# Held-back weight sums and the last turnings in the second product of a fused attention and feed-forward kernel

## Chip, core and metric

The kernel runs on one core of one Trainium2 chip. Its engines are TensorE (PE in the profile; PEld is its weight load), VectorE (DVE), ScalarE (ACT), GpSimd (POOL, "Pool" in the text) and SyncE (SP), which issues most DMAs. The metric is the device time of one execution in microseconds (us); the median over several executions is given. "Span" is the time that the profiler's record of one execution covers.

## What is computed

Hashed attention over 4 batches and 8 heads (768 positions, 64 numbers each), and then a feed-forward block on the 3072 rows of 512 numbers that come out. Only the second product of the feed-forward block bears on the change:

```python
def _moe_ref(x, w_in, w_out):            # x: 3072 x 512, from the attention
    h = x @ w_in                         # w_in: 512 x 2048
    g = h * (1.0 / (1.0 + np.exp(-1.702 * h)))
    return (g @ w_out).astype(np.float32)   # w_out: 2048 x 512
```

All inputs to these products are float32 (the weights come as float64 and are converted on the chip).

## The kernel before

**Stages.** Attention takes the first third of the span. Then `feed_forward` computes `x @ w_in` with the gelu (`hidden`, to about 614 us) and keeps the results in DRAM (`g_dram`), and then `g @ w_out`, from about 614 us to the end. The whole change lies in this last stage.

**Fewer multiplications.** Both products go by Strassen's scheme in Winograd's form, twice nested: a product of two 2 x 2 block matrices takes seven block products instead of eight, at the price of sums of blocks before and after. The outer scheme cuts `g @ w_out` into seven outer products, named by their number o in the order `OUTER = (1, 2, 6, 7, 5, 3, 4)`. The rows of x are taken in three super blocks of 1024 (`sb`), so the stage is a list `steps_out` of 21 products, counted n = 0 to 20 below. Each is again a product of two block matrices: seven inner products, each a group that shows as eight matmuls (128 x 256) in the trace and goes into one bank of PSUM, in the order 1, 2, 3, 6, 7, 5, 4 (in the last product 1, 3, 6, 7, 5, 2, 4). These groups are "L820" in the trace.

**Sums ahead of a product.** The scheme needs three sums and one overwritten block of each factor:

- of W_out: `inner_sums(at)` for the outer product OUTER[at], four sums (L211 to L214) of 128 x 512 on Pool. They are needed once, before product n = at; the products of the later super blocks use them again. The fourth result (L214) is the weight of inner product 3, the third group of its product. Those for at = 0 to 3 are made while `hidden` still runs; those for at = 4 to 6 during this stage.
- of g: `g_sums(n)`, four sums (L219 to L222) of 128 x 1024 on DVE, made during product n - 1 for product n: t1, then the block overwritten in place (raw_g or s_in), then t2, then t4. t2 is the moving factor of inner product 6, the fourth group (t2a for even n, t2b for odd n); t4 that of the last group.

**Sums behind a product.** `product_of_halves` (L809 to L853) emits the seven groups and takes their results out of PSUM: ScalarE copies groups 1 (`u`, L833) and 3 (L836), DVE adds the others (all adds are L824), and adds an earlier outer product's result where there is one (`acc`). Between them it calls `after(0)` to `after(3)` (`after(4)` in the last product alone), where the loop puts other work of DVE: pending additions and turnings, then the g sums of the next product: the first at 1, the second at 2, the last two at 3. For o = 3 an addition of two whole results (L957) comes ahead of the product, and another (L958) at `after(0)`.

**Turning and writing.** A finished result is turned in 32 x 32 blocks by DVE (`turned`, L800, one instruction for each of four quarters) into `y`, and `written` (L807) issues four DMAs from `y` to the output. In the last super block SP and ScalarE share these issues.

**Order.** The instructions of TensorE, DVE, ScalarE and Pool run in the order in which the code emits them; SP's order is set by a scheduler. The g blocks come by `fetch(n + 1)` (two DMAs of 1 MB on SP's queue, L775), issued during product n into the one of two buffers that product n - 1 has left.

**The marks.** Four times a copy of one element on Pool (L924) reads the result of the product before. It has no use for its value: Pool's queue waits there until that product's first DVE add is done, and so the sums behind it begin then:

```python
if 2 <= n <= 5:
    nc.gpsimd.tensor_copy(mark, ms[OUTER[n - 1]][0:1, 0, 0:1])
i = n % 2 * 2
for f in inner_sums(4) if n == 0 else inner_sums(4 + n // 2)[i : i + 2] if 2 <= n <= 5 else []:
    f()
```

So a mark emitted at n runs during product n - 1, and in the trace the marks of n = 2, 3, 4, 5 are at 637.46, 647.26, 658.06 and 669.18.

Of the kernel before, what the change touches and what calls it, by code (L numbers as in the profile page):

```python
# [38 lines left out]
def kernel(  # L39
# [113 lines left out]
    for x in (0x3FFFFFFF, 0xFF800000):  # L153
        m = const.tile([P, 1], U32, name=f"mask_{x:x}")
# [53 lines left out]
    def sums_a(eng, a11, a12, s3, a22, s1, s2, s4, a21=None):  # L208

        a21 = s3 if a21 is None else a21  # L210
        return [lambda: eng.tensor_tensor(s1, a21, a22, op=Alu.add),  # L211
                lambda: eng.tensor_tensor(s3, a11, a21, op=Alu.subtract),
                lambda: eng.tensor_tensor(s2, s1, a11, op=Alu.subtract),
                lambda: eng.tensor_tensor(s4, a12, s2, op=Alu.subtract)]  # L214
# [464 lines left out]
    def feed_forward(tag, late=()):  # L679
# [9 lines left out]
        with ExitStack() as fctx:  # L689
# [62 lines left out]
            def w_quarters(o):  # L752

                w = wqs[LEFT[o]]
                x = [w[:, i, F4 * j : F4 * (j + 1), :] for i in range(2) for j in range(2)]
                at = OUTER.index(o)
                if at == 0:
                    return x[0:2] + rooms[3:4] + x[3:] + rooms[0:3]
                return x + rooms[3 * at + 1 : 3 * at + 4]

            def inner_sums(at):

                if at == 0:
                    w = w_quarters(OUTER[0])
                    return sums_a(nc.gpsimd, *w, wqs[LEFT[OUTER[0]]][:, 1, 0:F4, :])
                return sums_a(nc.gpsimd, *w_quarters(OUTER[at])) if at < len(OUTER) else []
# [4 lines left out]
            def fetch(n):  # L771
                sb, o = steps_out[n]
                for h in range(2):
                    cs = slice(h * F4, (h + 1) * F4)
                    loader[0].dma_start(out=raw_g[n % 2][:, cs], in_=g_dram[len(LEFT) * sb + RIGHT[o], :, cs, :])  # L775
# [14 lines left out]
            def g_sums(n):  # L790
                return sums_b(nc.vector, *g_quarters(n)) if n < len(steps_out) else [lambda: None] * 4
# [3 lines left out]
            def turned(c, i, j, q0, q1):  # L795

                for q in range(q0, q1):
                    h, k = divmod(q, 2)
                    y = ys[j].rearrange("p b (d r) -> p r b d", r=4)[:, 2 * i + h, k * (TH // 32) : (k + 1) * (TH // 32), :]
                    nc.vector.transpose(y, c[:, q].rearrange("p (b t) -> p b t", t=32))  # L800

            def written(sb, j, halves, queues):
                first, last = halves[0] * TH, (halves[-1] + 1) * TH
                for a in range(4):
                    t0 = (2 * sb + j) * XT
                    dst = out[t0 + first : t0 + last, a * P : (a + 1) * P].rearrange("(b t) d -> t b d", t=32)
                    queues[a % len(queues)].dma_start(out=dst, in_=ys[j][32 * a : 32 * (a + 1), first // 32 : last // 32, :])  # L807

            def product_of_halves(n, acc, after):  # L809

                sb, o = steps_out[n]
                wq, gq = w_quarters(o), g_quarters(n)
                m = wholes[n % len(wholes)]
                u, v = (gp.tile([P, TH], F32, tag=x, name=x, bufs=2) for x in ("u", "v"))
                c11, c12, c21, c22 = (m[:, i] for i in range(4))

                def product(i):
                    ps = bank()[:, 0:TH]
                    for c in range(F4):
                        nc.tensor.matmul(ps, wq[LEFT[i]][:, c, :], gq[RIGHT[i]][:, c, :], start=(c == 0), stop=(c == F4 - 1))  # L820
                    return ps

                def add(dst, x, y):
                    nc.vector.tensor_tensor(dst, x, y, op=Alu.add)  # L824

                def corner():
                    add(c11, product(2), u)
                    if acc is not None:
                        add(c11, c11, acc[:, 0])


                final = n + 1 == len(steps_out)
                nc.scalar.copy(u, product(1))  # L833
                if not final:
                    corner()
                nc.scalar.copy(c12, product(3))  # L836
                after(0)
                add(v, product(6), u)
                add(c21, product(7), v)
                if acc is not None:  # L840
                    add(v, v, acc[:, 1])
                    add(c22, c21, acc[:, 3])
                    add(c21, c21, acc[:, 2])
                add(c12, c12, v)
                after(1)
                p = product(5)
                add(c22, p, c21 if acc is None else c22)
                add(c12, p, c12)
                after(2)
                if final:  # L850
                    corner()
                    after(4)
                add(c21, product(4), c21)  # L853
                after(3)
                return m

            def conversions(cv, psum, chunks):

                gens = [convert(cv, *x, psum=psum) for x in chunks]
                next(gens[0])  # L860
                for i, x in enumerate(gens):
                    for y in gens[i + 1 : i + 2]:
                        next(y)
                    for at, _ in enumerate(x):
                        if at == 2:
                            yield
                    yield

            MT = FC // 2
            for sb in range(n1):  # L870
                for mt in range(MT):
                    n = sb * MT + mt
                    if n == 1:
# [12 lines left out]
                        steps = conversions(cv, cps, late + chunks)  # L886
# [31 lines left out]
            for n, (sb, o) in enumerate(steps_out):  # L918
                final = n + 1 == len(steps_out)
                if 0 < n and n + 1 < len(steps_out):  # L920
                    fetch(n + 1)

                if 2 <= n <= 5:
                    nc.gpsimd.tensor_copy(mark, ms[OUTER[n - 1]][0:1, 0, 0:1])  # L924
                i = n % 2 * 2
                for f in inner_sums(4) if n == 0 else inner_sums(4 + n // 2)[i : i + 2] if 2 <= n <= 5 else []:
                    f()
                later_sums = g_sums(n + 1)
                m = wholes[n % len(wholes)]

                def after(at):
                    if at == 0:
                        while pending:
                            pending.pop(0)()

                    for f in later_sums[at : at + 1] if n == 0 else ([], later_sums[0:1], later_sums[1:2], later_sums[2:], [])[at]:
                        f()

                    if n + 2 >= len(steps_out):
                        for q in ((0,) * (not final), (), (1, 3), (2,), (0,))[at]:  # L940
                            turned(m, int(final), int(not final), q, q + 1)
                    if final and at in (2, 3):
                        written(sb, 0, (3 - at,), loader + [nc.scalar])
                    if n + 2 == len(steps_out) and at == 3:
                        written(sb, 1, (0, 1), loader + [nc.scalar])

                acc = {6: 1, 7: 6, 2: 1, 3: 6, 4: 7}.get(o)
                if o == 3:
                    pending.pop(0)()
                ms[o] = product_of_halves(n, None if acc is None else ms[acc], after)  # L950

                def flat(x):
                    return x.rearrange("p q t -> p (q t)")

                if o == 5:
                    m5, m6, m7 = (ms[i] for i in (5, 6, 7))
                    pending += [lambda a=m6, b=m5: nc.vector.tensor_tensor(flat(a), flat(a), flat(b), op=Alu.add),  # L957
                                lambda a=m5, b=m7: nc.vector.tensor_tensor(flat(a), flat(a), flat(b), op=Alu.add),  # L958
                                lambda a=m5: turned(a, 1, 1, 0, 4)]
                elif o in (2, 3) and n + 2 < len(steps_out):  # L960
                    pending.append(lambda a=ms[o], j=int(o == 3): turned(a, 0, j, 0, 4))
                    if o == 3:
                        pending.append(lambda sb=sb: written(sb, 1, (0, 1), loader))
                elif o == 4 and not final:
                    pending.append(lambda a=ms[4]: turned(a, 1, 0, 0, 4))
                    pending.append(lambda sb=sb: written(sb, 0, (0, 1), loader))
                yield
# [50 lines left out]
```

## Time and profile before

| what | value |
|---|---|
| median of 9 runs | 880.59 us (880.21 to 882.77) |
| profiled execution | 880.64 us, its span 878.8 us, granted TensorE clock 0.997 |
| busy over the span | PE 99%, DVE 82%, Pool 37%, ACT 36% |
| busy in 640 to 680 us | PE 38.05 of 40, DVE 33.22, Pool 8.46 |
| busy in 680 to 840 us | PE 160.00 of 160, DVE 128.85, Pool 0 |
| busy in 840 to 860 us | PE 20.00 of 20, DVE 17.74 |
| granted clock from 614 to 872 us | 1.00 |

A timeline line reads: start, duration, engine, line of the code, operation, output<-inputs, partitions x elements of output and input, how many such instructions in a row, and in brackets how long the engine had been idle before it and what ended that. Where a line merges several instructions ("x2"), the duration is from the first one's start to the last one's end. An instruction's record begins when its engine takes it up, so a duration can hold time in which it stands still. DMA issues are written with a q behind the engine (SPq, ACTq).

From 614 us TensorE's matmuls follow one another with two gaps, of 1.95 us and 0.82 us. A product of seven groups takes 12.09 us without a gap, a group 1.73 us. DVE's free durations in this stage are 1.22 us for a sum of 128 x 1024, 0.42 us for an add of 128 x 256, and 2.04 us for four transposes in a row; Pool's is 1.26 us for a sum of 128 x 512.

### The profile page before, as it was taken

The page shows a single profiled execution, that of the slowest core. Times are in us where ns is not written, and L with a number is a line of the kernel's source. Part 1 is how long each engine was busy: PE and PEld are TensorE (multiplying, and loading weights), DVE is VectorE, ACT ScalarE, POOL GpSimd, SP SyncE. Part 2 cuts the span into 40 slices and gives each one's busy share as a digit, 9 for nine tenths or more (in the row PEclk, how much of TensorE's full clock was granted, in tenths as well). Part 3 has the DMA queues.
Part 4 walks back from the last instruction along what each step waited for, and adds up shares of the span by engine and source line. Part 5 has one row for each costly group of instructions (what it writes and reads, how often), then busy time and mean ns, then how long its engine had stood idle before and what let it go on. Part 6 is the DMA issues. An engine that isn't in the chain of part 4 may idle for free.

```text
span 878.8 us, 11897 instructions
## 1 busy us (share of the span) xinstructions
PE 866.8 (99%) x4077; PEld 498.0 (57%) x4077; DVE 723.4 (82%) x1020; ACT 314.5 (36%) x519; POOL 322.1 (37%) x277
## 2 busy tenths in 40 slices
PE   9999999999999999999999999999999999999996
PEld 4444444444444444444444444444878888888885
DVE  4689989999999986787777787888897977897786
ACT  5767776776676642222232222332000000000000
POOL 4343343334433364675443344659931000000000
PEclk9999999999999999999999999999999999999998
DMA  6544545664444103555455645575835675467524
GB/s 132 95 62 85 104 82 99 100 102 84 83 82 97 56 0 133 214 195 203 165 186 197 215 163 196 199 246 178 303 133 187 200 219 209 157 221 239 192 96 100
DMA packets 169157, 132.01 MB, mean 150 GB/s; under 512 B 123616, under 2 KB 138112, under 8 KB 163712
## 3 DMA queue, kind: packets, MB, share of 16 engines
q1 hardware_dynamic: 166528, 129.70, 51.6%
q10 hardware_dynamic: 2560, 1.46, 0.8%
q8 instruction: 34, 0.56, 0.3%
q14 instruction: 35, 0.29, 0.1%
HBM read 79.69 MB, written 50.33 MB: 148 GB/s over the span
## 4 chain that ended last, share of the span: by engine, by line
PE 95%; DVE 4%; issue 0%; DVEq 0%
PE product L708 33%; PE product L820 25%; PE ps L432 18%; PE av L458 15%; PE dn L479 2%; DVE xT L824 2%; PE hash L408 1%; DVE y L800 1%; PE tp L366 1%; PE warm L359 0%; PE hash L373 0%; DVE v L824 0%; DVE t2a L221 0%; DVE raw_g L220 0%; DVE t4g L222 0%
## 5 line engine op out<-in xcount | busy, mean ns | idle before, releaser
L433 ACT ACTIVATE e<-ps 128x768 f32<-128x768 f32 x192 | 151.1, 812 | 15.0 <-PE ps L432 12.7
L432 PE MATMUL ps<-qT,kT 64*128 64x384 f32 x768 | 155.1, 482 | 0.0
L708 PE MATMUL product<-xT,w_in_sb 128*128 128x512 f32 x288 | 135.5, 593 | 0.0
L458 PE MATMUL av<-e,v 128*64 128x385 f32 x768 | 131.5, 490 | 0.0
L440 POOL TENSOR_TENSOR acc<-e 128x768 f32<-128x768 f32 x32 | 58.7, 1833 | 192.1 <-DVE acc L448 128.0
L716 ACT ACTIVATE c<-c 128x512 f32<-128x512 f32 x72 | 45.4, 630 | 186.9 <-issue 78.9
L458 PEld LDWEIGHTS av<-e,v 128*64 128x64 f32 x768 | 52.2, 136 | 76.4 <-issue 75.9
L708 PEld LDWEIGHTS product<-xT,w_in_sb 128*128 128x128 f32 x288 | 54.6, 190 | 69.1 <-issue 64.1
L708 PE MATMUL product<-t_x,s_in 128*128 128x512 f32 x192 | 90.2, 592 | 0.0
L432 PEld LDWEIGHTS ps<-qT,kT 64*128 64x128 f32 x768 | 68.1, 188 | 35.3 <-issue 35.3
L219 POOL TENSOR_TENSOR v<-c,u 128x512 f32<-128x512 f32 x24 | 34.2, 1424 | 123.2 <-ACT c L716 123.2
L833 ACT COPY u<-product 128x256 f32<-128x256 f32 x21 | 7.8, 372 | 173.9 <-PE product L820 132.3
L432 PE MATMUL ps<-qf,kf 64*128 64x384 bf16 x384 | 62.9, 324 | 0.1
L708 PEld LDWEIGHTS product<-t_x,s_in 128*128 128x128 f32 x192 | 36.5, 190 | 45.9 <-issue 43.8
L441 POOL TENSOR_TENSOR acc<-acc,e 128x768 f32<-128x768 f32 x32 | 59.1, 1847 | 2.5
L708 PE MATMUL product<-t_x,w_in_sb 128*128 128x512 f32 x96 | 45.1, 592 | 0.0
L708 PE MATMUL product<-xT,s_in 128*128 128x512 f32 x96 | 45.1, 592 | 0.0
L432 PEld LDWEIGHTS <-kf 64*128 64x128 bf16 x384 | 18.8, 94 | 41.3 <-issue 19.5
L446 DVE SCALAR_TENSOR_TENSOR acc<-e 128x768 f32<-128x768 f32 x32 | 32.2, 1007 | 5.1 <-ACT e L433 5.1
L469 ACT COPY vs<-av 128x1 f32<-128x1 f32 x32 | 5.1, 159 | 86.1 <-PE av L458 86.1
L820 PE MATMUL product<-raw_g,xT 128*128 128x256 f32 x152 | 35.1, 379 | 0.0
L448 DVE TENSOR_TENSOR acc<-acc,e 128x768 f32<-128x768 f32 x32 | 32.3, 1010 | 3.3
(208 smaller groups left out, 1543.6 us busy)
## 6 DMA issues: line engine op xcount, KB each, us to landing
raw_g<-g_dram SPq DMA_DIRECT2D x22, 1024.0 KB
s_in<-g_dram SPq DMA_DIRECT2D x20, 1024.0 KB
g_dram<-c SPq DMA_DIRECT2D x72, 256.0 KB
g_dram<-t SPq DMA_DIRECT2D x48, 256.0 KB
raw<-in_moe_w_in_dram SPq DMA_DIRECT2D x16, 512.0 KB
raw<-in_moe_w_out_dram SPq DMA_DIRECT2D x16, 512.0 KB
v<-in_v_dram SPq DMA_DIRECT2D x32, 192.0 KB
g_dram<-u SPq DMA_DIRECT2D x24, 256.0 KB
```

The costliest lines, as they stand in the source:

```text
L219: return [lambda: eng.tensor_tensor(t1, b12, b11, op=Alu.subtract), lambda: eng.tensor_tensor(b12, b22, b12, op=Alu.subtract), lambda: eng ...
L432: nc.tensor.matmul(ps[:, j, 0:HS], a[hs, keys], m[hs, cols], start=not last, stop=last)
L433: nc.scalar.activation(es[c][:, kt, :, 0:HS], ps[:, :, 0:HS], Act.Exp, scale=1.0 / D**0.5)
L440: nc.gpsimd.tensor_tensor(acc, es[c][:, 0, :, 0:HS], es[c][:, 1, :, 0:HS], op=Alu.add)
L441: nc.gpsimd.tensor_tensor(acc, acc, es[c][:, 2, :, 0:HS], op=Alu.add)
L446: nc.vector.scalar_tensor_tensor(acc, e[0], T * TINY, e[1], op0=Alu.add, op1=Alu.add)
L448: nc.vector.tensor_tensor(acc, acc, x, op=Alu.add)
L458: nc.tensor.matmul(av[D * j : D * (j + 1), :], vt[:, t, j, :], es[c][:, t, j, :], start=(t == 0), stop=(t == T - 1))
L479: nc.tensor.matmul(dn[r0 : r0 + 32, :], ones[:, 0:32], acc[:, j, :], start=True, stop=True)
L708: nc.tensor.matmul(ps, wq[LEFT[i]][:, kc, :], xq[RIGHT[i]][:, kc, :], start=(kc == 0), stop=(kc == K2 - 1))
L716: nc.scalar.activation(c, c, Act.Gelu_apprx_sigmoid)
L820: nc.tensor.matmul(ps, wq[LEFT[i]][:, c, :], gq[RIGHT[i]][:, c, :], start=(c == 0), stop=(c == F4 - 1))
```

## The change

```diff
-                if 2 <= n <= 5:
+                if n in (5, 6):
                     nc.gpsimd.tensor_copy(mark, ms[OUTER[n - 1]][0:1, 0, 0:1])
-                i = n % 2 * 2
-                for f in inner_sums(4) if n == 0 else inner_sums(4 + n // 2)[i : i + 2] if 2 <= n <= 5 else []:
+                for f in {0: inner_sums(4), 5: inner_sums(5) + inner_sums(6)[:2], 6: inner_sums(6)[2:]}.get(n, []):
                     f()
...
-                    for f in later_sums[at : at + 1] if n == 0 else ([], later_sums[0:1], later_sums[1:2], later_sums[2:], [])[at]:
-                        f()
+                    steps = [later_sums[at : at + 1]] if n == 0 else [[], later_sums[0:1], later_sums[1:2], later_sums[2:], []][at : at + 1]
+
+                    if n + 2 >= len(steps_out):
+                        turns = [lambda q=q: turned(m, int(final), int(not final), q, q + 1) for q in range(4)]
+                        if final:
+                            steps = [[[], [], [turns[1], turns[3]], [turns[2]], [turns[0]]][at]]
+                        elif at == 3:
+                            steps = [later_sums[2:3], turns[0:2], turns[3:4], later_sums[3:], turns[2:3]]
+                    for f in sum(steps, []):
+                        f()
 
-                    if n + 2 >= len(steps_out):
-                        for q in ((0,) * (not final), (), (1, 3), (2,), (0,))[at]:
-                            turned(m, int(final), int(not final), q, q + 1)
```

Two parts:

1. On Pool. The sums for OUTER[5] and OUTER[6] were made in pairs behind the marks of n = 2, 3, 4, 5. Now six of the eight stand behind the mark of n = 5 and the last two behind a mark of n = 6. The marks of n = 2, 3 and 4 are gone. The sums themselves are the same.
2. On DVE, in product 19 (the second but last). Its four turnings stood at `after(0)` (quarter 0), `after(2)` behind the second g sum (quarters 1 and 3), and `after(3)` behind the last g sum (quarter 2). Now all four are at `after(3)`: the third g sum (t2), quarters 0, 1 and 3, the fourth g sum (t4), quarter 2. The last product's turnings stay where they were.

The order of TensorE, ScalarE and SP is the same in both kernels.

## The prediction

> The products of the last stage are counted n = 0 to 20. Times with two decimals are microseconds from the start of the profiled span (878.8 us). Its execution took 880.64 us, so 1.8 us lie around the span; the median of the nine runs is 880.59, 0.05 lower.
>
> **What bounds the kernel now.** First the chain of waits, in order of time (start, us, engine):
>
> ```profile
> 613.99 20.73 PE product L820 x96
> ...
> 645.15 0.14 issue
> 645.29 197.09 PE product L820 x912
> ...
> 871.58 0.63 DVE y L800
> ```
>
> TensorE carries it, except from 634.7 to 645.3 and from 842.4 to the end, where it runs through DVE. TensorE's timeline prices both stretches:
>
> ```profile
> 645.29 1.97 PE L820 MATMUL product<-t2a,w_in_sb 128*128 128x256 f32 x8 [1.95 <-DVE t2a L221]
> ...
> 693.71 1.89 PE L820 MATMUL product<-t2a,s_in 128*128 128x256 f32 x8
> ...
> 862.19 1.99 PE L820 MATMUL product<-t2a,s_in 128*128 128x256 f32 x8 [0.82 <-DVE t2a L221]
> ```
>
> The first and third are TensorE's only waits in this stage. A product of seven groups takes 12.09 us (652.27 to 664.36); product 2 began at 638.00 and product 3 at 652.27, so the first wait costs 14.27 - 12.09 = 2.18. Around the other, groups begin at 859.47 and 864.02, 4.55 apart instead of 2 x 1.73: 1.09. Why t2a came late in product 2 is read from DVE's timeline and Pool's side by side:
>
> ```profile
> 636.31 3.02 DVE L824 TENSOR_TENSOR xT<-xT 128x256 f32<-128x256 f32 x2
> 639.26 1.49 DVE L824 TENSOR_TENSOR xT<-xT,v 128x256 f32<-128x256 f32 x1
> ...
> 643.94 1.21 DVE L221 TENSOR_TENSOR t2a<-raw_g,t1a 128x1024 f32<-128x1024 f32 x1
> ...
> 690.48 1.22 DVE L221 TENSOR_TENSOR t2a<-raw_g,t1a 128x1024 f32<-128x1024 f32 x1
> ```
>
> ```profile
> 636.18 1.33 POOL L214 TENSOR_TENSOR w_in_sb<-xT,w_in_sb 128x512 f32<-128x512 f32 x1
> 637.46 0.37 POOL L924 COPY mark<-xT 1x1 f32<-1x1 f32 x1
> 637.79 1.25 POOL L211 TENSOR_TENSOR w_in_sb<-xT 128x512 f32<-128x512 f32 x1
> 639.13 1.33 POOL L212 TENSOR_TENSOR xT<-xT 128x512 f32<-128x512 f32 x1
> ...
> 669.18 0.17 POOL L924 COPY mark<-t_x 1x1 f32<-1x1 f32 x1 [8.38 <-DVE t_x L824]
> ```
>
> The pair of adds at 636.31 took 3.02; the same pair at 650.33, with Pool idle, took 0.88. Each add ends about 0.3 after a Pool sum ends (637.51, 639.04, 640.46): a DVE sum of two SBUF tensors stands still while a Pool sum runs. It goes both ways: at 625.57 a Pool sum took 2.13 instead of 1.26, ending 1.27 after the DVE sum before it. They take turns, one whole instruction each. DVE adds that read a product from PSUM do not wait (the pair at 626.50: 0.74), nor do transposes (four at 647.12 beside two sums: 2.06; alone 2.04).
>
> **Part 1, the held-back sums.** Removed: two sums and a mark ahead of each of products 2, 3, 4, so with the added one four marks become two. The mark of product 5 stays and now leads six sums instead of two; a mark of product 6 with two sums is added. No DMA is issued more or less, and neither SP's nor ScalarE's order changes.
>
> Gain at product 2. L214 still ends at 637.51 and holds the first add; then Pool is empty. From the first add's end (637.85) the next ones go at their free pace: they start as if the pair had begun at 637.43, plus 0.79 (650.33 to 651.12), plus 0.34 (651.12 to 651.46), so t1a starts at 638.56 instead of 640.67, 2.11 earlier, and t2a ends at 645.15 - 2.11 = 643.04. TensorE wants it at 641.45 + 1.73 = 643.18 and takes it 0.06 to 0.14 after its end. The 2.18 go to 0, at most 0.1. From here all of TensorE is 2.18 earlier; DVE has waits for it of 1.38 and 1.30 in product 3, so it follows. The sums taken from 647.40 and 658.20 lay beside transposes and idle time, so taking them away is worth nothing.
>
> Cost at products 4 to 6. The mark now at 669.18 comes at 667.00. Six sums at a spacing of 1.30 start at 667.14, 668.47, 669.70, 671.04, 672.28, 673.62. DVE is idle or reading PSUM until 671.35, so three and a half sums are hidden by its waits of 2.35 and 1.30. Without that cover each costs up to 1.26. Then they take turns: the add c12 (673.53 before, now 671.35) waits for the fourth sum until 672.30; t1b waits for the fifth until 673.75 and ends 674.83; L220 waits for the sixth until 676.00 and ends 677.08, where it would have ended at 676.89 - 2.18 = 674.71. DVE is 2.37 late. The t2b wanted in product 5 at 681.62 - 2.18 = 679.44 ends at 678.35 - 2.18 + 2.37 = 678.54: in time. In product 5 the second mark waits for c11 (681.8); its two sums meet L958, which has already begun, and then transposes, so DVE loses nothing; they end by 685.4. DVE's only reserve there is its wait of 0.30 before 685.28. With it, DVE is back at the times it had before, and t2a of product 6 ends at 691.70 as now. But TensorE wants it at 693.71 - 2.18 = 691.53: a new wait of about 0.3, with the refill seen at 645.29 (1.97 instead of 1.89) 0.4. In product 7 DVE's idle 1.30 before 697.37 makes up the rest. Behind the marks only sums are queued, and TensorE waits for those: product 5 reads its fourth at 679.90 - 2.18 = 677.7 (done 672.3), product 6 its fourth at about 690 (done 685.4). One fetch is to be watched: the second half for product 8 stands in SP's queue behind four writes that wait for transposes, and these do not move; issued at 699.66, it is used at 710.13, then at 708.3; transfers run until about 706.3, so 2 us remain.
>
> Bounds of the new wait: nothing if Pool's sums start 0.4 earlier or DVE gains one turn; 1.8 if DVE loses the rest of all three sums, 3.8 in place of 2.37. I take 0.4, from the row-by-row turns.
>
> The Trainium skill speaks against bunching the sums: "SBUF — State Buffer", section "Who interferes with whom", has DVE instructions with two SBUF inputs contend with Pool's reads, whoever issues first holding the port for the whole instruction. The rows above agree on that lock, but show it changing hands after each instruction, which the page does not promise; if Pool kept it through its queue, the estimate would be 1.8 instead of 0.4.
>
> **Part 2, the turning of product 19.** Four transposes stay four. One of them leaves the batch of five at 851.92, two leave the place before t2a (859.66, 1.09 us); three come behind t2a. What DVE gains ahead of t2a: the batch of four frees v at 851.92 + 1.87 = 853.79 (1.87: 682.71 to 684.58) instead of 854.25, but the next add waits for its product until 854.50 (now 854.79), so 0.29; then 0.95 for the two (859.66 to 860.61): t2a ends near 860.92, before the 861.20 at which TensorE wants it. The 1.09 vanish from TensorE. But they do not reach the end, which ScalarE's timeline shows:
>
> ```profile
> 864.02 0.91 ACTq L807 DMA_DIRECT2D out_dram<-y  x2
> 865.03 0.37 ACT L833 COPY u<-product 128x256 f32<-128x256 f32 x1 [13.62 <-PE product L820]
> ```
>
> ScalarE copies u, the last product's first group, only after it has issued product 19's two writes, which wait for its last transpose; DVE's v at 865.43 waits for u. After that DVE runs to 872.21 with hardly a gap (0.1, for the group ending at 871.09). In the new order t2a at 859.70, three transposes at 0.47, t4 (1.14) and one transpose of 0.64 end at 864.14 instead of 863.95. So v comes at 865.62, and without the gap of 0.1 DVE ends at 872.3: +0.08. TensorE's 1.09 is hidden behind DVE. Bounds: -1.09 if the end followed TensorE; +0.4 if the writes, which keep the DMA engines at 0.9 and more from 865 to 875, pass their delay on twice. I take +0.1.
>
> **Sum.** 880.64 - 2.18 + 0.4 + 0.1 = 878.96; less 0.05 for the median: 878.9.
>
> **The rivals.**
> 1. No second wait: t2a of product 6 is in time. For it: 0.3 is small beside eight steps each known to 0.1. Against: DVE's chain from 671 to 691 has only 0.30 of idle. 880.6 - 2.18 + 0.1 = 878.5. Chance 0.15.
> 2. The end follows TensorE, u being out of the way: a further 1.09 + 0.1, so 877.7. Against: the order in ScalarE's queue is unchanged. 0.06.
> 3. Pool keeps the port: DVE 3.8 late, the new wait 1.8: 880.3, no change. For it: 3.02 at 636.31. Against: Pool's 2.13 at 625.57. 0.13.
> 4. Slower: the bunched sums hold DVE through products 4 to 6. If all eight block it in full, 8 x 1.26 = 10.1, less 0.30 of idle, it is 9.8 late; of this 1.87 is free at 691.70 (693.71 - 691.70 - 0.14), so the wait is 7.9: 880.6 - 2.2 + 7.9 + 0.1 = 886.4. It decides from the point where DVE is 5.8 late (1.87 + 2.18 + 1.76). For it: six sums in a row; against: half of them fall into idle time. 0.06.
>
> **How the numbers follow.** The forecast has 0.60; its own range, 878.3 to 879.6, comes from 0.1 to 0.9 for the new wait and 0 to 0.4 for the tail. A difference under 0.2% (1.76 us) is about what a measurement of this kernel can't tell from no change; the border is 878.83, and the forecast lies on it, so I split it in halves. Faster: 0.30 + 0.15 + 0.06 = 0.51. Within 0.2%: 0.30 + 0.13 = 0.43. Slower: 0.06. The range 878.0 to 880.3 leaves out most of rivals 2 and 4.
>
> **What would show it.** Right: no wait of TensorE near 643; the pair at 636.31 at about 1.9 us; six Pool sums from 667, the last three drawn out by DVE's; a short wait for t2a near 691.5; none near 861; DVE's v near the end still waiting for ScalarE's u. Wrong: a wait over 1 us between 675 and 705, or u copied before the writes are issued.

## The result, and the profile after

| | before | changed |
|---|---|---|
| median of the executions | 881.08 us (33 runs, 879.87 to 883.34) | 878.7 us (10 runs, 878.32 to 879.53) |
| ratio, 95% interval | | 0.997 (0.9962 to 0.9978) |
| profiled execution, span | 880.64 us, 878.8 us | 878.69 us, 876.9 us |
| first group of product 0 to u of product 19 | 233.81 us | 232.02 us |
| u of product 19 to the end of DVE's last instruction | 24.58 us | 24.48 us |
| from there to the end of the span | 6.59 us | 6.41 us |

The last three rows split the span behind the start of the stage into "stage", "tail" and "rest", which are used for all experiments below. In the changed kernel, profiled a second time, they are 232.03, 24.47 and 6.42. Between kernels that do not differ there, stage and tail repeat to 0.03 us; the rest repeats less well, it lies between 6.25 and 6.45 in eight profiles with the same order of turning and writing. Two executions far outside all others (1140.29 us of part 1 alone, at a granted clock of 0.753, and 3949.94 us of the kernel before) are left out everywhere. The stage is read from the start of the first L820 group to ScalarE's copy L833 in product 19, the tail from that copy to the end of the last L800. So the profile's 1.9 us are 1.79 of stage, 0.10 of tail and 0.18 of rest, less 0.17 by which this execution reached the stage later.

The chain of waits of the changed kernel, in order of time:

```profile
614.15 77.75 PE product L820 x360
691.90 0.12 issue
692.02 160.83 PE product L820 x744
...
862.43 0.37 ACTq L807
...
863.44 0.38 ACT u L833
...
869.86 0.63 DVE y L800
```

From 614 to 692 TensorE now carries it without DVE; what is left of a wait stands at 692. At the end ScalarE's DMA issues (ACTq) and its copy of u have come into the chain. TensorE's timeline at the three places where the prediction looked:

```profile
643.34 1.94 PE L820 MATMUL product<-t2a,w_in_sb 128*128 128x256 f32 x8
...
690.01 1.89 PE L820 MATMUL product<-raw_g,s_in 128*128 128x256 f32 x8
692.02 1.96 PE L820 MATMUL product<-t2a,s_in 128*128 128x256 f32 x8
...
859.58 1.89 PE L820 MATMUL product<-t2a,s_in 128*128 128x256 f32 x8
```

No bracket is left: the waits of 1.95 and 0.82 us are gone. A small one has come: after 690.01 the next group was due at 691.74 and starts at 692.02, and it takes 1.96 instead of 1.89. Product 2 now takes 650.29 - 638.16 = 12.13 us, product 6 takes 699.00 - 686.55 = 12.45, 0.36 over the free 12.09. DVE and Pool of the changed kernel, first where the wait was, then where the six sums meet DVE:

```profile
636.48 1.95 DVE L824 TENSOR_TENSOR xT<-xT 128x256 f32<-128x256 f32 x2
638.35 0.42 DVE L824 TENSOR_TENSOR xT<-xT,v 128x256 f32<-128x256 f32 x1
...
671.56 1.25 DVE L824 TENSOR_TENSOR t_x<-t_x,v 128x256 f32<-128x256 f32 x1
672.73 2.28 DVE L219 TENSOR_TENSOR t1b<-s_in 128x1024 f32<-128x1024 f32 x1
674.93 0.74 DVE L824 TENSOR_TENSOR t_x<-product,t_x 128x256 f32<-128x256 f32 x2
675.60 1.62 DVE L220 TENSOR_TENSOR s_in<-s_in 128x1024 f32<-128x1024 f32 x1
...
690.66 1.22 DVE L221 TENSOR_TENSOR t2a<-raw_g,t1a 128x1024 f32<-128x1024 f32 x1
```

```profile
667.21 0.17 POOL L924 COPY mark<-t_x 1x1 f32<-1x1 f32 x1 [29.51 <-DVE t_x L824]
...
671.26 1.26 POOL L214 TENSOR_TENSOR w_in_sb<-xT,w_in_sb 128x512 f32<-128x512 f32 x1
672.48 1.44 POOL L211 TENSOR_TENSOR w_in_sb<-w_out_sb 128x512 f32<-128x512 f32 x1
674.00 2.14 POOL L212 TENSOR_TENSOR w_out_sb<-w_out_sb 128x512 f32<-128x512 f32 x1
681.94 1.11 POOL L924 COPY mark<-t_x 1x1 f32<-1x1 f32 x1 [5.80 <-DVE t_x L824]
```

Read the ends: Pool's fourth sum ends at 672.52 and DVE's add at 672.81, Pool's fifth at 673.92 and t1b at 675.01, Pool's sixth at 676.14 and L220 at 677.22. The two engines take turns, one instruction each, while the adds at 674.93, which read PSUM, keep their 0.74.

The tail: first DVE's v in the kernel before, then DVE and ScalarE of the changed kernel:

```profile
865.43 0.42 DVE L824 TENSOR_TENSOR v<-product,u 128x256 f32<-128x256 f32 x1 [1.49 <-ACT u L833]
```

```profile
859.20 1.58 DVE L800 STREAM_TRANSPOSE y<-xT 128x256 f32<-128x256 f32 x3
...
863.85 0.43 DVE L824 TENSOR_TENSOR v<-product,u 128x256 f32<-128x256 f32 x1 [1.49 <-ACT u L833]
```

```profile
862.43 0.91 ACTq L807 DMA_DIRECT2D out_dram<-y  x2
863.44 0.37 ACT L833 COPY u<-product 128x256 f32<-128x256 f32 x1 [13.65 <-PE product L820]
```

The group that u is copied from has been ready since about 858, for 5 us. The copy waits behind two writes, these for the last turning (861.75 to 862.36), and DVE for the copy, for the same 1.49 us as before. TensorE's last group ends at 868.38, 2.1 us ahead of DVE (before: 1.1).

### The profile page after: what moved, and what is told of

Read it like the earlier page. It is cut to its first block, busy times and chain, and to the rows that moved or that the text cites. A ratio compares the mean times of both kernels' runs of the same rounds, so it can differ in the third digit from the quotient of the medians.

```text
span 876.9 us, 11895 instructions
## 1 busy us (share of the span) xinstructions
PE 866.4 (99%) x4077; PEld 497.8 (57%) x4077; DVE 723.1 (82%) x1020; ACT 314.8 (36%) x519; POOL 323.8 (37%) x275
## 4 chain that ended last, share of the span: by engine, by line
PE 96%; DVE 2%; DMA 1%; issue 0%; SPq 0%; ACTq 0%; ACT 0%; DVEq 0%
PE product L708 33%; PE product L820 27%; PE ps L432 18%; PE av L458 15%; PE dn L479 2%; PE hash L408 1%; DVE xT L824 1%; DMA q<-in_q_dram 1%; DVE y L800 1%; PE hash L373 0%; PE tp L366 0%; DVE v L824 0%; DVE t2a L221 0%; DVE raw_g L220 0%; ACTq L807 0%
## 5 line engine op out<-in xcount | busy, mean ns | idle before, releaser
L833 ACT COPY u<-product 128x256 f32<-128x256 f32 x21 | 7.8, 372 | 172.1 <-PE product L820 138.9
L820 PE MATMUL product<-raw_g,xT 128*128 128x256 f32 x152 | 35.1, 379 | 0.0
```

## The experiments

Every time in the lists "stage, tail, rest" is from one profile; before: 233.81, 24.58, 6.59, changed: 232.02, 24.48, 6.41.

**Each part alone.** The two parts of the diff do not touch each other's lines, so each was put into the kernel before by itself.

> The kernel before with the first part alone (Pool's sums in products 5 and 6; product 19 turned as before). Theory A (the whole gain is product 2's wait, less a new one in product 6): no wait of TensorE in product 2, about 0.3 us of wait ahead of inner product 6 of product 6, and the old wait of about 0.8 us in the last product; 1.7 to 1.9 us faster than before, so the same time as the changed kernel within 0.3 us. Theory B (part 2 carries a share of the gain): at least 0.5 us slower than the changed kernel.

> The kernel before with the second part alone (product 19 turned behind three of the last product's sums; Pool's sums as before). Theory A (ScalarE copies u only behind the two writes it issues, and these wait for the last turning): no wait of TensorE in the last product, but DVE's first add of inner product 6 there still waits for u and ends the chain; the span changes by less than 0.3 us. Theory B: TensorE's wait of 1.09 us reaches the end, 0.8 to 1.2 us faster than before.

Part 1 alone: 232.02, 24.57, 6.73; ratio to the kernel before 0.9971 (0.996 to 0.9983), that of the whole change within 0.0001. TensorE waits 0.81 us in the last product, as before, and 0.28 in product 6. Theory A holds.

Part 2 alone: 235.51, 24.48, 6.45; ratio 0.9999 (0.9987 to 1.0011). No wait of TensorE in the last product, and no gain of 0.8 us or more in the executions: theory B falls. The span of the profiled execution was to change by less than 0.3 us, but it is 2.0 us longer (880.8 against 878.8): it reached the stage 0.54 us later, and its stage, which part 2 does not touch, is 1.70 us longer. TensorE's timeline and the windows of one microsecond (the last three columns are granted clock, DMA share and GB/s) show why:

```profile
645.84 2.67 PE L820 MATMUL product<-t2a,w_in_sb 128*128 128x256 f32 x8 [1.96 <-DVE t2a L221]
648.30 2.92 PE L820 MATMUL product<-raw_g,xT 128*128 128x256 f32 x8
```

```profile
646.00:647.00 1.00, 1.00 (x5) 0.87 (x5) 1.00 (x2) 0.00 (x0) 0.00 (x0) 0.98 0.00 0
647.00:648.00 1.00, 1.00 (x4) 0.80 (x3) 0.97 (x3) 0.00 (x0) 0.19 (x2) 0.50 0.07 8
...
650.00:651.00 1.00, 1.00 (x5) 0.88 (x4) 0.00 (x0) 0.00 (x0) 0.57 (x1) 0.82 0.97 410
651.00:652.00 1.00, 1.00 (x7) 0.87 (x6) 0.71 (x2) 0.00 (x0) 0.00 (x0) 1.00 0.18 74
```

After the same wait of 1.96 us the granted clock falls to 0.50 from about 647.0 to 650.4. The clock lost in 646 to 651 is 0.02 + 3 x 0.50 + 0.18 = 1.70 us, the whole of the difference. In the kernel before's own profile it stays at 1.00 there. Six of part 2's twelve executions took over 881.9 us, against nine of the kernel before's 26 in the same rounds; the medians of those below are 880.03 and 880.36.

**Where the first pair stands.**

```diff
-                if n in (5, 6):
+                if n in (2, 5, 6):
...
-                for f in {0: inner_sums(4), 5: inner_sums(5) + inner_sums(6)[:2], 6: inner_sums(6)[2:]}.get(n, []):
+                for f in {0: inner_sums(4), 2: inner_sums(5)[:2], 5: inner_sums(5)[2:] + inner_sums(6)[:2], 6: inner_sums(6)[2:]}.get(n, []):
```

The other version has 4 in place of 2 in both lines.

> The changed kernel with the first two of the held-back sums back behind a mark of n = 2; the other six stay at n = 5 and 6. Theory A (these two sums alone hold DVE up in product 2): the wait of 1.9 us ahead of inner product 6 of product 2 is back, the wait in product 6 is gone since only four sums run from 669 on; 880.4 to 880.8 in one profile, as before the change. Rival (it is the marks, or the sums of n = 3 and 4, that cost): no wait in product 2, time as the changed kernel's.

> The changed kernel with the first two of the held-back sums behind a mark of n = 4, so that four instead of six stand behind that of n = 5. Theory A (DVE is late in product 6 because the last three of six bunched sums meet its own sums): DVE is about 0.9 instead of 2.0 us late after product 4's sums, no wait of TensorE in products 2 to 7, 0.3 to 0.4 us faster than the changed kernel. Rival (the wait in product 6 comes from the two sums behind the mark of n = 6, or from the late transposes): the wait of 0.3 us stays, and the time is the changed kernel's.

The pair at n = 2: 233.82, 24.46, 6.37, the stage of the kernel before to 0.01. The wait of product 2 is back, that of product 6 gone (its t2a group starts 1.73 after the one ahead of it):

```profile
645.13 1.97 PE L820 MATMUL product<-t2a,w_in_sb 128*128 128x256 f32 x8 [1.96 <-DVE t2a L221]
```

Ratio 0.9992 (0.9982 to 1.0001). The profiled execution, 880.13 us, is 0.3 under the range that I gave; its stage is as expected, and the rest lies outside it (0.17 ahead of the stage, 0.12 in the tail, 0.22 behind it).

The pair at n = 4: 231.66, 24.48, 6.38; ratio 0.997 (0.9959 to 0.9982). With four sums instead of six, DVE's add c12 still waits for the fourth, but t1b finds Pool idle:

```profile
671.15 1.24 DVE L824 TENSOR_TENSOR t_x<-t_x,v 128x256 f32<-128x256 f32 x1
672.32 1.21 DVE L219 TENSOR_TENSOR t1b<-s_in 128x1024 f32<-128x1024 f32 x1
```

DVE needs 4.43 us from c12 to t2b (671.15 to 675.58), where the changed kernel needs 5.92 and the kernel before 3.60: 0.83 late instead of 2.32. TensorE has no wait left, and the stage is 0.36 us shorter than the changed kernel's: the second wait comes from the bunched sums, and this is its price.

**The mark without sums.** The version above, with one more mark, at n = 2 (`if n in (2, 4, 5, 6):`).

> The version with the first pair of sums at n = 4, with one more mark at n = 2 and no sums behind it. Theory A (the two sums, not the mark, hold DVE up in product 2): no wait of TensorE in product 2 beyond 0.2 us, time as the version without that mark, 877.9 to 878.6. Rival (the mark itself costs): a wait of 0.4 us or more in product 2.

231.67, 24.46, 6.35, no wait: it is the sums that cost, not the mark. The four executions have a median of 878.12 us.

**The copy of u ahead of the writes.** The changed kernel with product 19's writes moved into the last product's `after(0)`:

```diff
                         while pending:
                             pending.pop(0)()
+                        if final:
+                            written(sb, 1, (0, 1), loader + [nc.scalar])
...
-                    if n + 2 == len(steps_out) and at == 3:
-                        written(sb, 1, (0, 1), loader + [nc.scalar])
```

> The changed kernel with product 19's writes issued in the last product after ScalarE has copied u and the third group, instead of ahead of these copies. Theory A (the copy of u behind the writes is what keeps TensorE's 1.09 us from the end): DVE's add at 863.85 no longer waits for ScalarE, DVE ends 0.9 to 1.1 us earlier (869.5 instead of 870.5). The span follows by 1.0 us if the transfers had room, or by only 0.3 to 0.5 us if they set the end, since the DMA engines are busy from 863.3 to 874.3 but for 0.35 us at 868. Rival (something else holds the tail): no change.

232.02, 23.49, 6.76. DVE's v starts at 862.64 straight behind the turning and no longer waits for ScalarE; the tail is 0.99 us shorter, as forecast. But 0.35 of it comes back in the rest. The transfers would explain it: they run without a break until after 873, though the computation is over at 870; the version in halves below bears on this.

```profile
868.00:869.00 1.00, 0.81 (x4) 0.38 (x2) 0.97 (x3) 0.00 (x0) 0.00 (x0) 1.00 0.94 173
...
872.00:873.00 1.00, 0.00 (x0) 0.00 (x0) 0.00 (x0) 0.00 (x0) 0.00 (x0) 0.50 1.03 260
873.00:874.00 1.00, 0.00 (x0) 0.00 (x0) 0.00 (x0) 0.00 (x0) 0.00 (x0) 0.50 0.51 143
```

In the changed kernel the last column but one, the DMA share, dips to 0.65 at 868. So 0.64 us reach the end in this profile, between the two values expected. Ratio 0.9963 (0.995 to 0.9977).

**Both, and then in halves.** The pair at n = 4 together with the writes behind the copies; and that with quarters 1 and 3 of product 19 turned first and written first:

```diff
-                            written(sb, 1, (0, 1), loader + [nc.scalar])
+                            written(sb, 1, (1,), loader + [nc.scalar])
+                            written(sb, 1, (0,), loader + [nc.scalar])
...
-                            steps = [later_sums[2:3], turns[0:2], turns[3:4], later_sums[3:], turns[2:3]]
+                            steps = [later_sums[2:3], turns[1:2], turns[3:4], turns[0:1], later_sums[3:], turns[2:3]]
```

> The two edits that are expected to gain, together: the first pair of the held-back sums at n = 4, and product 19's writes behind the copies of u and the third group. If the gains add: 0.4 us for the first and 0.4 to 1.0 us for the second below the changed kernel, 877.2 to 877.9.

> The version before this one, with product 19's quarters 1 and 3 turned first and that half written by four DMAs of its own, the other half by four more. If transfers set the end of the version before: their start comes forward by about 1.5 us and the end follows DVE's last transpose, a further 0.4 to 0.6 us faster. If DVE sets it already: no further gain, or up to 0.3 us lost to four more DMA issues on each of the two queues.

Together: 231.66, 23.50, 6.57, median 877.6 us, ratio 0.9959 (0.9946 to 0.9971): the gains add. Of the 0.98 us of tail 0.79 reach the end here (24.48 + 6.38 against 23.50 + 6.57). In halves: 231.65, 23.49, 6.40, median 876.85 us, ratio 0.9952 (0.9939 to 0.9964). The transfers start between 860 and 861 instead of at 863 and come to a stop before the last ones:

```profile
865.00:866.00 1.00, 1.00 (x6) 0.87 (x5) 0.97 (x3) 0.00 (x0) 0.00 (x0) 1.00 0.28 72
866.00:867.00 1.00, 1.00 (x6) 0.89 (x5) 0.97 (x3) 0.00 (x0) 0.00 (x0) 1.00 0.00 0
```

So the rest is back at 6.40 (6.42 in a second profile), which fits the transfers having held the end, though 0.17 us lie within what the rest varies by. The profiles show 0.17 us for this step, less than I expected, the medians 0.75; six runs each don't settle what lies between. Both this version and the changed kernel ran again in the same rounds:

> The changed kernel once more, on the same chip and in the same rounds as the next: 878.3 to 879.5 as before.

> The fastest version (first pair of sums at n = 4, product 19 written in halves behind the copies of u and the third group) beside the changed kernel: 876.6 to 877.7, some 1.7 us faster than it.

878.83 us (878.6 to 879.38) and 876.98 us (876.69 to 877.5), with ratios to the kernel before of 0.9969 (0.9956 to 0.9981) and 0.9946 (0.9932 to 0.996): 1.85 us apart. This version beats both kernels.

**The clock after a gap.** To see whether the wait brings the clock down, it was made longer: four, then six sums behind the mark of n = 2 (`2: inner_sums(5)`, and `2: inner_sums(5) + inner_sums(6)[:2]`).

> The changed kernel with four of the held-back sums behind a mark of n = 2 (and two each at n = 5 and 6), to make the wait in product 2 longer: two more turns taken from DVE, t2a 1.7 us later, TensorE's gap about 3.6 instead of 1.95 us, so 882.2 to 882.6 by the waits alone. Theory C (a gap of that length makes the TensorE clock fall to half for some 3.3 us, as the profile of the second part alone shows after its gap of 1.96 us, and a longer gap does so more often): most executions 1.5 to 2 us above that, 884 to 884.5, the clock 0.5 in some of the microseconds after the gap. Rival (the clock's fall in that one profile has nothing to do with the gap): executions near 882.4, with the same share of outliers as the kernel before.

> Six of the held-back sums behind a mark of n = 2, two behind that of n = 6, to make TensorE's gap in product 2 longer still: 4.5 to 5.0 us, by the waits alone 1.1 to 1.6 us above the 881.8 that the version with four took at a full clock, 882.9 to 883.4. Theory C (a gap lets the TensorE clock fall to half): in nearly all executions at least 1.5 us more, 884.5 and above, and this profile shows a clock of 0.5 for about 3 us after the gap. Rival (no link): most executions near 883.

With four, the gap is 3.44 us:

```profile
646.67 1.97 PE L820 MATMUL product<-t2a,w_in_sb 128*128 128x256 f32 x8 [3.44 <-DVE t2a L221]
```

The profiled execution kept its full clock and took 881.8 us (a stage of 235.29), 0.4 under the range, the gap being a little shorter than I had worked out. Of the twelve executions (881.29 to 885.76, median 883.42), ten took at least 1.0 us more than that one, though only five reached 884; none of the ten was profiled, and some are up to 4.0 us slower, more than the 1.70 of one fall of the clock. With six, the gap is 4.18 us, not 4.5, and all five executions took 884.35 to 885.93. Its profile, the gap's end and the windows behind it:

```profile
647.75 3.42 PE L820 MATMUL product<-t2a,w_in_sb 128*128 128x256 f32 x8 [4.18 <-DVE t2a L221]
```

```profile
648.00:649.00 1.00, 1.00 (x4) 0.80 (x4) 1.00 (x1) 0.00 (x0) 0.73 (x1) 0.55 0.00 0
649.00:650.00 1.00, 1.00 (x4) 0.82 (x3) 1.00 (x2) 0.00 (x0) 0.00 (x0) 0.50 0.00 0
...
651.00:652.00 1.00, 1.00 (x5) 0.86 (x4) 1.00 (x4) 0.00 (x0) 0.00 (x0) 0.75 0.91 205
```

Lost again: 0.45 + 0.50 + 0.50 + 0.25 = 1.70 us. The stage is 237.72, 3.91 over that of the kernel before: 2.23 from the longer gap (4.18 - 1.95), 1.70 from the clock. This supports theory C without settling it. In all fourteen profiles, the granted clock from 300 us to the end of the last matmul, in slices of 5 us, is below 1.00 only in these two, and in both the fall follows the gap. The fall comes late: counted from the gap's start it begins after 3.1 us with part 2 alone and after 4.5 us with six sums. That agrees with the end of the kernel, where matmuls stop for good and the clock begins to fall to half between 2.1 and 4.8 us later in all fourteen profiles. But the pair at n = 2 has the same gap of 1.96 us and only one of its twelve executions above 881.9 us, so the length of the gap alone does not set how often it costs more.

## Why the prediction was right, and where it was off

Predicted 878.9 us, measured 878.7.

- **The wait of product 2** (2.18 to 0, at most 0.1): measured 12.13 - 12.09, so 0.04 is left, and 2.14 gained. The pair of adds took 1.95, forecast "about 1.9". Moving two sums back to n = 2 brings back the stage of the kernel before to 0.01 us; a mark alone does not. Shown.
- **The turns of product 4.** L220 was to end at 677.08; in this profile, whose stage starts 0.17 later, it ends at 677.22. DVE was to be 2.37 late and is 2.32. In the prediction's rows for the kernel before two readings are a little off, without effect on the sum: the Pool sum at 625.57 ends 1.12, not 1.27, after the DVE sum (624.29 + 2.29), and the DMA share drops to 0.60 at 870.
- **The new wait of product 6** (0.4): 0.36. Part of this agreement is luck: 2.37 late less the reserve of 0.30 is 2.07, which the prediction took as 2.18; but the reserve was worth only 0.17 (t2b starts 0.35 later than before, t2a 0.18), so t2a ended where it was said to. Four sums instead of six take it away (stage -0.36). Rival 1, no second wait, falls by as much; rivals 3 and 4, Pool keeping the port or all eight sums blocking, fall with the turns seen at 672 to 677. One detail differs: it is the second mark itself that stands still for L958 (L961 in the changed kernel; 1.11 instead of 0.17), not the sum behind it; the sums then lie beside the transposes as forecast.
- **Part 2 doesn't bring TensorE's 1.09 us to the end.** Held: part 2 alone has ratio 0.9999, v still waits for u. Rival 2 falls for this kernel, and the version that copies u first shows what it lacked: 0.99 us of tail, of which 0.64 and 0.79 reach the end in two profiles.
- **The tail's size** (+0.1, the term that was mis-sized): measured -0.10 in DVE and -0.18 in the rest. In DVE I took 1.25 us from the start of t2a to the first transpose, read where the transposes turn what the instruction ahead of them wrote; here it is 1.13, and v comes 0.15 earlier than worked out. Tail and rest together are 31.17 and 31.30 in the two profiles without part 2 and 30.73 to 30.93 in the eight that have it with the writes in their old place, so part 2 may be worth some 0.2 to 0.6 us. The lower executions of part 2 alone point the same way (880.03 against 880.36), but part 1 alone and both parts have the same ratio (0.9971 and 0.997). How much part 2 is worth, and why the rest is shorter, stays open.
- **What the sum did not hold: the price of the wait in executions other than the profiled one.** The prediction took 2.18 from one profile and set 0.05 between profile and median. Of the kernel before's 85 executions in all comparisons, 33 took 881.9 us or more (median 882.59) and 52 took 881.6 or less (median 880.6); no changed-kernel execution of 16 exceeded 879.53. The 2.0 us between the medians of the groups are near the 1.70 of the clock. That these 33 had their clock halved is not shown, since none of them was profiled; where the mean clock is listed for each execution, it is 0.9964 in the upper and 0.9976 in the lower group (20 and 32 of them), which makes 0.0012 x 881 = 1.1 us and leaves the remainder open. So against the lower group the change is worth 1.9 us, near the 1.7 of the prediction's sum, and against the median of 881.08 it is 2.4.

## What to carry to other kernels

Before moving work on one engine, lay it beside the other engine's instructions and work through the turns by hand: here each Pool sum next to a DVE sum of two SBUF tensors cost its whole remaining length, and next to idle time, transposes or PSUM reads nothing. A wait removed upstream is worth only what the end of the chain can use: look at what the last engine waits for, here a copy of 0.37 us standing behind two DMA issues. And price a wait of TensorE over many executions: in one profile here a wait of 1.96 us was followed by a loss of 1.70 us of clock, in two others by none.

## What the runs showed of the hardware

In one profile a TensorE gap of 1.96 us was followed by a granted clock of 0.50 for 3.4 us, which began after the matmuls had resumed (645.84, and from 647.0) and cost 1.70 us; the same gap left the clock at 1.00 in the profiles of the kernel before and of the pair at n = 2, as did one gap of 3.44; after one of 4.18 it was halved from 0.4 us after the gap's end, and none of that kernel's five executions was below 884.35 us. The Trainium skill, "TensorE: Matmul & The Clock Gate", section "Part 1: The HAM clock gate", tells of a free-running window of about 3.4 us, and its section "Why this matters for your kernels" advises against idle gaps over some 3 us. The length of the half-speed stretch and its coming in one profile and not in another agree with such a window; the limit does not agree with the one profile in which a gap of 1.96 us was followed by the fall.
